# A transformer block on one core: a ninth unit of maxima beside the projections, no fourth bank of maxima in the attention, two V tiles later, five buffers of V rows

## The chip, the core and the metric

The kernel runs on one core of a Trainium2 chip. The core has a matrix engine (TensorE, PE in the profile; PEld is its weight load), a vector engine (VectorE, DVE), an activation engine (ScalarE, ACT), a general engine (GpSimd, POOL), and SyncE (SP), which here issues DMA transfers. ScalarE's queue issues a few more. The metric is the device time of one execution in microseconds (us); less is better.

## The reference

A transformer block over x of 2048 tokens by 512, with 32 heads of 16 and a feed-forward width of 1792, all in float32:

```python
def _A_ref(x, wqkv, wo):                       # attention
    qkv = (x @ wqkv).reshape(B, S, 3, H, Dh).transpose(2, 0, 3, 1, 4)
    q, k, v = qkv[0], qkv[1], qkv[2]
    scores = jnp.einsum("bhqd,bhkd->bhqk", q, k) * Dh ** -0.5
    p = softmax(scores, axis=-1)
    o = jnp.einsum("bhqk,bhkd->bhqd", p, v)
    return o.transpose(0, 2, 1, 3).reshape(B, S, D) @ wo

def _B_ref(x, w1, b1, w2, b2):                 # feed-forward
    return gelu(x @ w1 + b1) @ w2 + b2

mod = (silu(c) @ w_mod).reshape(c.shape[0], 6, 1, -1)
sa, ca, ga, sb, cb, gb = (mod[:, i] for i in range(6))
h = layernorm(x) * (1 + ca) + sa
x = x + ga * _A_ref(h, A_wqkv, A_wo)
h = layernorm(x) * (1 + cb) + sb
x = x + gb * _B_ref(h, B_w1, B_b1, B_w2, B_b2)
```

The softmax needs the largest score of each row of queries before its exponentials.

## The kernel before

Every engine works through its own list in the order in which the code writes it down. A product of two float32 matrices is made from high and low parts, in three terms (`mm3`, L284 to L292): 12 matmuls for a tile of 128 by 512.

**Stages.** The loop over four blocks of 512 tokens (L504 to L538) is the first part. In each block it normalises the next block (`ln1`, `ln1_t`), projects K and then Q for the first quarter of the heads (`proj_qk` with k = 0), and projects V tiles in between (`proj_v`). Block 0 takes four V tiles, blocks 1 and 2 two each, one before and one after the transposes of `ln1_t`. The second part (L547 to L602) is a list of 32 items: the eight V tiles that are left (n = 0 to 7), then K and Q for k = 1 to 3 over the four blocks. The attention (L819 to L844) follows, and then the feed-forward part.

**Units and maxima.** A unit is one group of four heads (of 8 groups) and one block of queries: 32 units, u = 4 g + block. Each unit needs 64 banks of maxima before its own scores can be made. There are two ways to get them.

- In the second part, `visit` (L556) makes two slots of `pair_slot` (L405). The keys of tokens t and t + 512 are held as their sum and their difference (`kpm`), so that the larger of two scores is half of a sum and an absolute value. A V slot makes two matmuls and two absolute values on ScalarE (L424); a U slot makes two matmuls and two VectorE instructions that add and keep the maximum (L428). From item 6 (`FILL0`) each item calls `visit` five times between its matmuls. `NU1` = 8 units are made so, in 256 slots.
- In the attention, `next_max` (L455) makes one bank by a matmul (L400) and a VectorE reduction (L402). The bank comes from the ring `mx` of three banks.

**A step of the attention.** A unit has 16 steps over the keys, kc = 0 to 15. A step has four score matmuls with their exponentials (X, L816 and L817, from the ring `sc` of four banks), the PV matmuls of the step before (P, L649, into the single bank `pv`), and three banks of maxima (M), in one of two orders (`ORDER`, L43). At kc = 4 and 12 (`EXTRA`, L45) a fourth bank is put in, and it is taken from the ring `sc`. The last unit makes no maxima.

**The sums of K.** `proj_qk` makes them for k = 0 alone (L305 to L322): of an even block ScalarE keeps a copy of K (`k2`); of the odd block VectorE makes sum and difference (`pm`), ScalarE the high parts (`pmh`), and, in `rest`, GpSimd the low parts, and two stores go to DRAM. `rest` also stores the projection's own parts, and is called after the next projection's matmuls. Its stores are issued by `st[0]`: ScalarE's queue until item 1 of the second part, SP's from there.

**K tiles and queues.** Four SBUF tiles hold keys: kt0, kt1, kq0, kq1. In the second part kt0 and kt1 first hold the sums of groups 0 and 1 (`build_k` of `kpm_d`, six loads each; half of kt0's are issued at block 3's start and half after the first part). kq0 is loaded with group 0 at item 10. At item 20 kt0 is loaded with group 2, which the attention's first maxima need; kt1 takes group 1 and kq1 group 3 after the last item. `load_qm` loads a unit's queries for the maxima, `load_q` for the scores. `max_rows` sends a finished unit's maxima to DRAM one item or step later (four stores). All of these go through SP's queue in the order of the code.

**V rows.** ScalarE writes a V tile into one of three buffers `vst` (L332, L333), and `rest` stores it to DRAM.

Of the kernel before, what the change touches and what calls it, by code (L numbers as in the profile page):

```python
# [16 lines left out]
P = 128  # L17
# [17 lines left out]
NU1 = 8  # L35
# [9 lines left out]
EXTRA = {4: "m0", 12: "m1"}  # L45
# [5 lines left out]
def block_kernel(ctx: ExitStack, tc: tile.TileContext, x, wqkv, wo, w1, b1, w2, b2, c, w_mod, out):  # L51
# [39 lines left out]
    kpm_d = dram.tile([2, P, S], F32, name="kpm")  # L91
# [33 lines left out]
    vst = [vwpool.tile([P, NG, VG], F32, name=f"vst{i}") for i in range(3)]  # L125
# [171 lines left out]
    def proj_qk(b, k, w, fill=()):  # L297
        hi, lo = hT[b]
        ps = bank()
        mm3(ps, [w_hi[k][:, w, i] for i in range(KC)], [w_lo[k][:, w, i] for i in range(KC)],  # L300
            [hi[:, i] for i in range(KC)], [lo[:, i] for i in range(KC)], fill)
        parts = tpool.tile([P, 2, TB], FR, tag="parts", name="parts", bufs=4)
        ac.activation(parts[:, 0], ps, AF.Copy)
        ve.tensor_tensor(parts[:, 1], ps, parts[:, 0].bitcast(F32), op=ALU.subtract)
        pair = w and k == 0  # L305
        if pair and b % 2 == 0:
            k2[0] = apool.tile([P, TB], F32, tag="k2", name="k2")
            ac.activation(k2[0], ps, AF.Copy)
        if pair and b % 2:
            pm = [apool.tile([P, TB], F32, tag="h32", name="pm", bufs=3) for _ in range(2)]  # L310
            pmh = [tpool.tile([P, 2, TB], FR, tag="parts", name="pmh", bufs=4) for _ in range(2)]
            for i, op in enumerate((ALU.add, ALU.subtract)):
                ve.tensor_tensor(pm[i], ps, k2[0], op=op)
                ac.activation(pmh[i][:, 0], pm[i], AF.Copy)

        def rest():
            st[0].dma_start(qk_d[w][k][:, :, b * TB : (b + 1) * TB].rearrange("a p t -> p a t"), parts.bitcast(F32))
            if pair and b % 2:
                for i in range(2):
                    gp.tensor_tensor(pmh[i][:, 1], pm[i], pmh[i][:, 0].bitcast(F32), op=ALU.subtract)  # L320
                    t0 = (b - 1 + i) * TB
                    st[0].dma_start(kpm_d[:, :, t0 : t0 + TB].rearrange("a p t -> p a t"), pmh[i].bitcast(F32))  # L322

        return rest
# [67 lines left out]
    def max_bank(u, i, a, bk):  # L392
# [6 lines left out]
        ps = bk()  # L399
# [55 lines left out]
    def next_max(a, bk=bank_mx):  # L455

        u, i = divmod(mi[a], NM)
        if u == NG * NB:
            return []
        if i == 4 and u + 1 < NG * NB and u + 1 not in qmx:  # L460
            load_qm(u + 1)
        mi[a] += 1
        max_bank(u, i, a, bk)
        return [] if left[u] else [max_rows(u)]
# [39 lines left out]
    for b in range(NB):  # L504
        if b == NB - 1:
# [6 lines left out]
            build_k(kts[0], kpm_d, 0, 0, 2 * TB)  # L512
# [7 lines left out]
        proj(proj_qk, b, 0, 1)  # L520
        proj(proj_qk, b, 0, 0)
# [4 lines left out]
        proj(proj_v, *vitems.pop(0))  # L526
        ev = ln1_t(b + 1, xn)
        ev()
        proj(proj_v, *vitems.pop(0))
# [5 lines left out]
        if b == 0:  # L535
            proj(proj_v, *vitems.pop(0))
            proj(proj_v, *vitems.pop(0))
    build_k(kts[0], kpm_d, 0, 2 * TB, S)  # L538
# [23 lines left out]
    for n, (k, b, w) in enumerate(items):  # L562
# [3 lines left out]
        if n == 8:  # L566
            build_k(kts[1], kpm_d, 1)
# [12 lines left out]
        if n == nv + 12:  # L580
            load_k(2, kts[0])
# [10 lines left out]
        if n >= FILL0:  # L592
            fill = [lambda rest=rest: (rest(), visit())] + [visit] * 4
# [18 lines left out]
    load_k(1, kts[1])  # L612
# [206 lines left out]
    for s in range(NS):  # L819
# [5 lines left out]
        order = list(ORDER[s % 2])  # L825
        if kc in EXTRA:
            order.insert(2, EXTRA[kc])
        for tok in order if u < NU - 1 else ORDER_END:
# [5 lines left out]
            else:  # L834
                new += next_max(int(tok[1]), bank if tok[0] == "m" else bank_mx)
# [149 lines left out]
```

## Time and profile before

| | us |
|---|---|
| three runs | 1789.81, 1792.59, 1793.21 |
| median of the runs | 1792.59 |
| profiled execution, its own time | 1789.69 |
| span of the profiled execution | 1787.9 |
| first part, to the last matmul of block 3's Q | about 80.1 |
| six V tiles without maxima | 80.3 to 101.6 |
| 26 items with maxima | 101.6 to 293.3 |
| attention | 293.3 to about 1430 |
| feed-forward part | about 1430 to 1787.9 |

Busy time over the whole span: TensorE 1768.5 us (99%), VectorE 1436.3 (80%), ScalarE 1343.1 (75%), GpSimd 246.4 (14%). Shares over the whole span are means over stages with different limits, so a stage is read by its own windows. A row of a window gives the stretch, its length, each engine's busy time with the number of instructions, the clock that TensorE was granted (1.00 is full speed), the share of the DMA engines and what they moved. A row of the timeline gives start and length in us, engine, line, operation, what is written and read, and in brackets the engine's idle time before it and what ended that. Matmuls overlap, so their lengths are longer than their distance. A row SPq or ACTq is a queue that issues a transfer.

### The profile page before, as it was taken

The numbers are of one execution on the slowest core, as the hardware profiler recorded it, in microseconds if no ns is written. First come the engines' busy times: TensorE is split into PE (matmuls) and PEld (weight loads), VectorE is DVE, ScalarE is ACT, GpSimd is POOL, SyncE is SP. The second block draws the span as 40 slices with busy tenths as digits, with TensorE's granted clock in tenths as the row PEclk, the third lists the DMA queues.
The fourth block names the chain that finished last, engine by engine and source line by source line (L and its number), as shares of the span: only waits on it lengthen the run. The fifth ranks groups of instructions, "written<-read, shape, count | busy, mean of one in ns | idle before, by whom it ended". The sixth has DMA issues, their size and how long they took to land.

```text
span 1787.9 us, 29214 instructions
## 1 busy us (share of the span) xinstructions
PE 1768.5 (99%) x10554; PEld 917.2 (51%) x10554; DVE 1436.3 (80%) x2591; ACT 1343.1 (75%) x2552; POOL 246.4 (14%) x259
## 2 busy tenths in 40 slices
PE   8999999999999999999999999999999999999998
PEld 7755554434444434444444434434434478788887
DVE  6469999999898889898988988898897476838453
ACT  3468887999999999999999999999999722223222
POOL 3300000010000000000000000000002044546462
PEclk9999999999999999999999999999999999999999
DMA  8776445411300410400411101100113064333331
GB/s 282 243 149 152 94 137 106 90 35 44 64 23 24 78 28 23 80 28 22 73 26 31 38 23 28 44 23 17 35 51 105 30 183 135 124 82 107 106 118 47
DMA packets 122432, 139.97 MB, mean 78 GB/s; under 512 B 38736, under 2 KB 72528, under 8 KB 120528
## 3 DMA queue, kind: packets, MB, share of 16 engines
q1 hardware_dynamic: 117872, 129.10, 28.5%
q10 hardware_dynamic: 4416, 9.01, 1.4%
q8 instruction: 83, 1.36, 0.3%
q14 instruction: 61, 0.50, 0.1%
HBM read 104.28 MB, written 33.77 MB: 77 GB/s over the span
## 4 chain that ended last, share of the span: by engine, by line
PE 91%; DVE 3%; DMA 2%; issue 2%; POOL 1%; SPq 0%; ACT 0%; ACTq 0%; DVEq 0%; POOLq 0%
PE pv L649 28%; PE mx L400 20%; PE sc L816 14%; PE sc L290 14%; PE mx L883 5%; PE mx L417 5%; PE pv L883 2%; PE sc L756 1%; PE mx L756 1%; DVE glo L866 0%; POOL w2l L687 0%; PE sc L252 0%; DMA rb<-rden 0%; DMA qk<-parts 0%; DVE cp L428 0%
## 5 line engine op out<-in xcount | busy, mean ns | idle before, releaser
L817 ACT ACTIVATE p<-sc 128x512 f32<-128x512 f32 x2048 | 1054.8, 613 | 72.9 <-PE sc L816 43.0
L402 DVE TENSOR_REDUCE mxs<-mx 128x1 f32<-128x512 f32 x1475 | 934.3, 684 | 109.7 <-PE sc L816 73.6
L649 PE MATMUL pv<-p,vg 128*32 128x512 f32 x4096 | 546.8, 605 | 0.0
L816 PE MATMUL sc<-qst,kq 50*128 50x512 f32 x1024 | 294.7, 439 | 1.4 <-DVE mxf L428 1.4
L816 PE MATMUL sc<-qst,kt 50*128 50x512 f32 x1024 | 293.3, 435 | 0.0
L400 PE MATMUL mx<-kq,qmx 48*128 48x512 f32 x737 | 258.5, 429 | 0.2
L400 PE MATMUL mx<-kt,qmx 48*128 48x512 f32 x738 | 258.4, 428 | 0.1
L400 PEld LDWEIGHTS mx<-kt,qmx 48*128 48x128 f32 x738 | 122.4, 185 | 219.2 <-DVE mxs L402 200.6
L400 PEld LDWEIGHTS mx<-kq,qmx 48*128 48x128 f32 x737 | 121.7, 185 | 219.7 <-DVE mxs L402 199.4
L862 ACT ACTIVATE g<-sc,b_c 128x512 f32<-128x512 f32 x56 | 38.6, 690 | 237.2 <-PE sc L290 228.5
L428 DVE CUSTOM_DVE_ANT_0 cp<-mx,cp 128x512 f32<-128x512 f32 x256 | 164.0, 686 | 30.4 <-PE mx L417 26.1
L649 PEld LDWEIGHTS pv<-p,vg 128*32 128x32 f32 x4096 | 81.1, 108 | 173.0 <-issue 161.3
L441 POOL CAST m<-mn 128x16 fp32r<-128x16 f32 x32 | 6.5, 202 | 1174.8 <-DVE mn L435 1174.8
L424 ACT ACTIVATE cp<-mx 128x512 f32<-128x512 f32 x256 | 141.1, 597 | 32.6 <-PE mx L417 27.9
L816 PEld LDWEIGHTS sc<-qst,kq 50*128 50x128 f32 x1024 | 131.3, 185 | 40.6 <-ACT p L817 31.6
L816 PEld LDWEIGHTS sc<-qst,kt 50*128 50x128 f32 x1024 | 131.2, 185 | 20.7 <-ACT p L817 14.7
L866 DVE TENSOR_TENSOR glo<-g,ghi 128x512 fp32r<-128x512 f32 x56 | 60.0, 1072 | 94.8 <-ACT ghi L865 94.8
L417 PE MATMUL mx<-kt,qmx 48*128 48x512 f32 x512 | 100.7, 456 | 0.5 <-ACT cp L424 0.5
L685 POOL TENSOR_TENSOR w1l<-w1r,w1h 128x512 fp32r<-128x512 f32 x56 | 76.8, 1372 | 152.7 <-DVE w1h L684 151.2
L290 PE MATMUL sc<-hThi,w 128*128 128x512 f32 x256 | 83.6, 436 | 2.9 <-DVE hThi L258 2.9
L687 POOL TENSOR_TENSOR w2l<-w2r,w2h 128x512 fp32r<-128x512 f32 x56 | 81.2, 1449 | 6.5 <-DVE w2h L686 6.1
L417 PEld LDWEIGHTS mx<-kt,qmx 48*128 48x128 f32 x512 | 52.8, 184 | 50.6 <-issue 23.3
(150 smaller groups left out, 1694.5 us busy)
## 6 DMA issues: line engine op xcount, KB each, us to landing
w1r<-in_B_w_dram SPq DMA_DIRECT2D x56, 256.0 KB
w2r<-in_B_w_dram SPq DMA_DIRECT2D x56, 256.0 KB
qmx<-qk SPq DMA_DIRECT2D x192, 64.0 KB
qk<-parts SPq DMA_DIRECT2D x24, 512.0 KB
qst<-qk SPq DMA_DIRECT2D x192, 64.0 KB
wmod<-in_w_mod_dram SPq DMA_DIRECT2D x6, 1024.0 KB
kq<-qk SPq DMA_DIRECT2D x24, 256.0 KB
kt<-qk SPq DMA_DIRECT2D x24, 256.0 KB
```

Source lines behind the costliest of these rows:

```text
L290: te.matmul(ps, p, q, start=i == 0, stop=i == len(terms) - 1)
L400: te.matmul(ps, qmx[u][rows, p, qc * P : (qc + 1) * P], kst[u // NB][rows, p, kr * TB : (kr + 1) * TB], start=True, stop=True)
L402: ve.tensor_reduce(mxs[u][:, p, a, qc, kr : kr + 1], ps, axis=AX.X, op=ALU.max, negate=True)
L417: te.matmul(ps, qmx[u][rows, p, qc * P : (qc + 1) * P], kpm[u // NB][rows, p, t0 : t0 + TB], start=True, stop=True)
L424: ac.activation(vabs[n, a], ps, AF.Abs)
L428: ve.tensor_tensor_reduce(v, ps, v, -0.5, 3.0e38, ALU.add, ALU.min, mxs[u][:, p, a, qc, r : r + 1])
L649: te.matmul(cur_pv[0][32 * j : 32 * (j + 1)], vg[g][:, kc, j * VW : j * VW + 32], pt.pop((s, j)), start=kc == 0, stop=kc == NKC - 1)
L685: gp.tensor_tensor(alo, a, ahi.bitcast(F32), op=ALU.subtract)
L687: gp.tensor_tensor(blo, b, bhi.bitcast(F32), op=ALU.subtract)
L816: te.matmul(ps, k[r0 : r0 + KX, p, kc * P : (kc + 1) * P], q[r0 : r0 + KX, p], start=True, stop=True)
L817: ac.activation(pb, ps, AF.Exp, scale=SCALE)
L883: te.matmul(acc[qb][t], p[:, sl], q, start=f == 0 and n == 0, stop=f == NF - 1 and n == 2)
```

## The change

- `NU1` is 9: 288 slots in 144 visits. The extra calls of `visit` go to every item whose number is a multiple of 7, from 7 to 28. The last item spreads its visits as if there were two more.
- `EXTRA` and the bank argument are gone: each step of the attention has three maxima from `mx`.
- `V_A` gives block 0 three V tiles (one before the transposes, two after), block 1 two, block 2 one, after the transposes. The list of items grows to 34, ten of them V tiles, so all item numbers from `nv` move by two.
- `vst` has five buffers.
- `proj_qk` makes the sums of K for k = 0 and for k = 1. `kpm_d` becomes two DRAM tensors. `k2` and `pm` move to another pool with tags of their own.
- In block 3, K's `rest` runs at once, ahead of Q's projection, with its stores on SP's queue.
- kt0 is loaded with the sums of group 2 at item `nv` + 11 = 21, for unit 8. So group 2's own K goes into kt1, at item `nv` + 22 = 32, and group 1's into kt0 after the last item.

```diff
--- before.py
+++ after.py
@@ -32,7 +32,7 @@
 KR = 3 * DH
 KX = KR + 2
 NM = 32
-NU1 = 8
+NU1 = 9
 FILL0 = 6
 VISIT = 2
 OP0 = 1
@@ -42,7 +42,7 @@
 
 ORDER = ("X0 X1 M1 X2 M0 X3 P M1".split(), "X0 X1 X2 M0 M0 X3 P M1".split())
 
-EXTRA = {4: "m0", 12: "m1"}
+V_A = ((1, 2), (1, 1), (0, 1))
 ORDER_END = "X0 X1 X2 X3 P".split()
 SCALE = DH ** -0.5
 
@@ -88,7 +88,7 @@
 
     qk_d = [[dram.tile([2, P, S], F32, name=f"qk{w}{k}") for k in range(4)] for w in range(2)]
 
-    kpm_d = dram.tile([2, P, S], F32, name="kpm")
+    kpm_d = [dram.tile([2, P, S], F32, name=f"kpm{k}") for k in range(2)]
     o_d = [dram.tile([D, TB], F32, name=f"o{b}") for b in range(NB)]
     den_d = [dram.tile([H, TB], F32, name=f"den{b}") for b in range(NB)]
     rden_d = [dram.tile([H, TB], F32, name=f"rden{b}") for b in range(NB)]
@@ -122,7 +122,7 @@
     wslots = [wpool.tile([P, KC, D], FR, name=f"w{i}") for i in range(2)]
     vwcm, vwpool = pool("vwpool", side="right")
     vslots = [vwpool.tile([P, KC, D], FR, name=f"wv{i}") for i in range(2)]
-    vst = [vwpool.tile([P, NG, VG], F32, name=f"vst{i}") for i in range(3)]
+    vst = [vwpool.tile([P, NG, VG], F32, name=f"vst{i}") for i in range(5)]
     acm, apool = pool("apool", side="right")
     c_c = apool.tile([P, KC], F32, name="c_c")
     s_c = apool.tile([P, KC], F32, name="s_c")
@@ -302,15 +302,15 @@
         parts = tpool.tile([P, 2, TB], FR, tag="parts", name="parts", bufs=4)
         ac.activation(parts[:, 0], ps, AF.Copy)
         ve.tensor_tensor(parts[:, 1], ps, parts[:, 0].bitcast(F32), op=ALU.subtract)
-        pair = w and k == 0
+        pair = w and k < 2
         if pair and b % 2 == 0:
-            k2[0] = apool.tile([P, TB], F32, tag="k2", name="k2")
-            ac.activation(k2[0], ps, AF.Copy)
+            k2[k] = tpool.tile([P, TB], F32, tag="k2", name="k2", bufs=1)
+            ac.activation(k2[k], ps, AF.Copy)
         if pair and b % 2:
-            pm = [apool.tile([P, TB], F32, tag="h32", name="pm", bufs=3) for _ in range(2)]
+            pm = [tpool.tile([P, TB], F32, tag="pm", name="pm", bufs=2) for _ in range(2)]
             pmh = [tpool.tile([P, 2, TB], FR, tag="parts", name="pmh", bufs=4) for _ in range(2)]
             for i, op in enumerate((ALU.add, ALU.subtract)):
-                ve.tensor_tensor(pm[i], ps, k2[0], op=op)
+                ve.tensor_tensor(pm[i], ps, k2[k], op=op)
                 ac.activation(pmh[i][:, 0], pm[i], AF.Copy)
 
         def rest():
@@ -319,7 +319,7 @@
                 for i in range(2):
                     gp.tensor_tensor(pmh[i][:, 1], pm[i], pmh[i][:, 0].bitcast(F32), op=ALU.subtract)
                     t0 = (b - 1 + i) * TB
-                    st[0].dma_start(kpm_d[:, :, t0 : t0 + TB].rearrange("a p t -> p a t"), pmh[i].bitcast(F32))
+                    st[0].dma_start(kpm_d[k][:, :, t0 : t0 + TB].rearrange("a p t -> p a t"), pmh[i].bitcast(F32))
 
         return rest
 
@@ -389,14 +389,14 @@
 
     mi = [NU1 * NM, NU1 * NM]
 
-    def max_bank(u, i, a, bk):
+    def max_bank(u, i, a):
 
         if u not in left:
             mxs[u] = small.tile([P, 2, 2, 4, 4], F32, tag="mxs", name="mxs")
             left[u] = 2 * NM
         p, qc, kr = i // 16, (i // 4) % 4, i % 4
         rows = slice(a * 64, a * 64 + KR)
-        ps = bk()
+        ps = bank_mx()
         te.matmul(ps, qmx[u][rows, p, qc * P : (qc + 1) * P], kst[u // NB][rows, p, kr * TB : (kr + 1) * TB],
                   start=True, stop=True)
         ve.tensor_reduce(mxs[u][:, p, a, qc, kr : kr + 1], ps, axis=AX.X, op=ALU.max, negate=True)
@@ -452,7 +452,7 @@
 
         return rest
 
-    def next_max(a, bk=bank_mx):
+    def next_max(a):
 
         u, i = divmod(mi[a], NM)
         if u == NG * NB:
@@ -460,7 +460,7 @@
         if i == 4 and u + 1 < NG * NB and u + 1 not in qmx:
             load_qm(u + 1)
         mi[a] += 1
-        max_bank(u, i, a, bk)
+        max_bank(u, i, a)
         return [] if left[u] else [max_rows(u)]
 
 
@@ -509,7 +509,7 @@
             qmcm, qmpool = pool("qmpool")
             kpm[0], kpm[1] = kts
             load_qm(0)
-            build_k(kts[0], kpm_d, 0, 0, 2 * TB)
+            build_k(kts[0], kpm_d[0], 0, 0, 2 * TB)
         if b == 2:
             split_w(1)
             load_w(2)
@@ -518,24 +518,27 @@
         if b + 2 < NB:
             load_x(b + 2)
         proj(proj_qk, b, 0, 1)
+        if b == NB - 1:
+            st[0] = sy
+            rest()
+            rest, st[0] = lambda: None, ac
         proj(proj_qk, b, 0, 0)
         if b == NB - 1:
             break
         if b in (1, 2):
             mrow = mod_rows(wms)
-        proj(proj_v, *vitems.pop(0))
+        for _ in range(V_A[b][0]):
+            proj(proj_v, *vitems.pop(0))
         ev = ln1_t(b + 1, xn)
         ev()
-        proj(proj_v, *vitems.pop(0))
+        for _ in range(V_A[b][1]):
+            proj(proj_v, *vitems.pop(0))
         if b == 1:
             mod_cols(1, mrow)
             wms = [load_wm(2, 0), load_wm(5, 1)]
         if b == 2:
             mod_bcast((ga_b, gb_b), mrow)
-        if b == 0:
-            proj(proj_v, *vitems.pop(0))
-            proj(proj_v, *vitems.pop(0))
-    build_k(kts[0], kpm_d, 0, 2 * TB, S)
+    build_k(kts[0], kpm_d[0], 0, 2 * TB, S)
     open_psum(sc=2, mx=6)
 
     vg = {}
@@ -564,7 +567,7 @@
             close(acm)
             st[0] = sy
         if n == 8:
-            build_k(kts[1], kpm_d, 1)
+            build_k(kts[1], kpm_d[0], 1)
             for t in kts:
                 one_rows(t)
         if n == nv + 1:
@@ -577,8 +580,11 @@
         if n == nv + 2:
             load_k(0, kq[0])
             load_v(0)
-        if n == nv + 12:
-            load_k(2, kts[0])
+        if n == nv + 11:
+            kpm[2] = kts[0]
+            build_k(kts[0], kpm_d[1], 2)
+        if n == nv + 22:
+            load_k(2, kts[1])
         if n == nv + 18:
             load_q(0)
         if n == nv + 20:
@@ -590,7 +596,9 @@
         new = []
         fill = [rest]
         if n >= FILL0:
-            fill = [lambda rest=rest: (rest(), visit())] + [visit] * 4
+            fill = [lambda rest=rest: (rest(), visit())] + [visit] * (4 + (n % 7 == 0))
+        if n == len(items) - 1:
+            fill += [lambda: None] * 2
         rest = proj_qk(b, k, w, fill) if k else proj_v(b, w, fill)
         for f in todo[:1]:
             f()
@@ -609,7 +617,7 @@
     pcm, ppool = pool("ppool", bufs=2)
     kq.append(ppool.tile([P, 2, S], FR, name="kq1", bufs=1))
     one_rows(kq[1])
-    load_k(1, kts[1])
+    load_k(1, kts[0])
     load_k(3, kq[1])
     epool = ctx.enter_context(tc.tile_pool(name="epool", bufs=1, side="right"))
 
@@ -822,17 +830,14 @@
         if kc == 2 and 0 < u < NU - 1:
             load_q(u + 1)
         new = []
-        order = list(ORDER[s % 2])
-        if kc in EXTRA:
-            order.insert(2, EXTRA[kc])
-        for tok in order if u < NU - 1 else ORDER_END:
+        for tok in ORDER[s % 2] if u < NU - 1 else ORDER_END:
             if tok[0] == "X":
                 exp_step(s, int(tok[1]))
             elif tok[0] == "P":
                 if s:
                     pv_step(s - 1)
             else:
-                new += next_max(int(tok[1]), bank if tok[0] == "m" else bank_mx)
+                new += next_max(int(tok[1]))
         for f in todo[:1]:
             f()
         todo = todo[1:] + new
```

## The prediction

> **What bounds the kernel now.** I read the chain of waits first, then a table of windows by stage.
>
> ```profile
> PE 91%; DVE 3%; DMA 2%; issue 2%; POOL 1%; SPq 0%; ACT 0%; ACTq 0%; DVEq 0%; POOLq 0%
> PE pv L649 28%; PE mx L400 20%; PE sc L816 14%; PE sc L290 14%; PE mx L883 5%; PE mx L417 5%; PE pv L883 2%; PE sc L756 1%; PE mx L756 1%; DVE glo L866 0%; POOL w2l L687 0%; PE sc L252 0%; DMA rb<-rden 0%; DMA qk<-parts 0%; DVE cp L428 0%
> ```
>
> ```profile
> core 0: us, PE busy (x) PEld busy (x) DVE busy (x) ACT busy (x) POOL busy (x), PEclk, DMA share, GB/s
> 0.00:40.00 40.00, 34.61 (x178) 27.51 (x179) 26.58 (x58) 13.15 (x21) 14.31 (x34) 0.91 0.87 304
> 40.00:75.00 35.00, 34.32 (x179) 24.52 (x178) 19.31 (x42) 15.12 (x25) 11.53 (x10) 1.00 0.63 224
> 75.00:102.50 27.50, 24.67 (x100) 19.32 (x98) 2.58 (x4) 6.40 (x11) 3.21 (x3) 0.94 0.77 215
> 102.50:293.30 190.80, 188.93 (x823) 100.88 (x822) 179.95 (x550) 155.69 (x287) 8.01 (x18) 1.00 0.51 123
> 293.30:330.00 36.70, 36.56 (x237) 14.84 (x239) 31.50 (x52) 32.84 (x64) 0.42 (x2) 0.95 0.91 130
> 330.00:1360.00 1030.00, 1029.90 (x7084) 416.27 (x7080) 926.77 (x1518) 975.29 (x1904) 31.41 (x63) 1.00 0.18 39
> ```
>
> TensorE holds the end almost everywhere, with VectorE and ScalarE close behind (90% and 95% in the attention). So a stage is worth what its TensorE rhythm changes by. Four places matter: the first part (to 80.1 us), the six V tiles without maxima (80.3 to 101.6), the 26 items with maxima (to 293.3), and 31 of the attention's 32 units (to about 1395).
>
> The attention's rhythm is read from the starts of the PV matmuls in the timeline. One step holds a fourth bank:
>
> ```profile
> 601.46 1.06 PE L649 MATMUL pv<-p,vg 128*32 128x512 f32 x8
> ...
> 603.04 0.40 PE L400 MATMUL sc<-kq,qmx 48*128 48x512 f32 x1
> ...
> 603.68 0.18 PEld L816 LDWEIGHTS sc<-qst,kt 50*128 50x128 f32 x1 [0.37 <-ACT p L817]
> ...
> 604.11 1.06 PE L649 MATMUL pv<-p,vg 128*32 128x512 f32 x8
> ...
> 606.23 1.07 PE L649 MATMUL pv<-p,vg 128*32 128x512 f32 x8
> ...
> 608.34 1.07 PE L649 MATMUL pv<-p,vg 128*32 128x512 f32 x8
> ```
>
> A plain step takes 2.12 us (604.11 to 606.23 to 608.34), the one with the bank 2.65. The fourth maximum sits in one of the four score banks, so the last score matmul waits for ScalarE. Over the trace the median is 2.637 with it and 2.124 without: 0.513 us each.
>
> The stall among the six V tiles:
>
> ```profile
> 97.33 3.30 PE L290 MATMUL sc<-wv,hThi 128*128 128x512 f32 x8 [2.83 <-ACT vst L333]
> 100.43 1.52 PE L290 MATMUL sc<-wv,hTlo 128*128 128x512 f32 x4
> ```
>
> With three row buffers ScalarE waits 7.14 us for a V store, and TensorE stands for 2.83. Then it runs slowly: 3.30 and 1.52 us, where the tile before took 2.03 and 1.10.
>
> **The sum.**
>
> 1. *No fourth bank.* Steps 4 and 12 of 31 units lose it: 62 x 0.513 = **-31.8**. The regular slots carry it: 31 x 48 = 1488 for 23 x 64 = 1472 banks. Unit 31's last maximum comes 16 slots early (5.3 steps of 2.12, 11.3 us; before, 14 slots, about 10). Bounds: -15, if only a bank's own share of the chain returns (20% of 1787.9 over 1475 banks = 0.242 each), to -33. I take the measured difference of steps.
>
> 2. *Nine units.* 16 more visits and two more items in the second part. An item without maxima takes 2.80 us, one with five visits 7.38 on average (24 items, from 109.8 to 286.9), so a visit costs (7.38 - 2.80) / 5 = 0.916. 16 x 0.916 + 2 x 2.80 = **+20.3**. VectorE allows it: two maxima per visit start 0.61 apart, six visits and the split of 0.69 are 8.0, TensorE needs 8.3. Bounds: +19 (two more items at 7.38 and four extra visits, the empty visits of the old last item forgotten) to +24 (all at VectorE's mean of 1.47 a visit).
>
> 3. *Sums of K for k = 1.* Two items get two VectorE passes (L313, 682 ns each as x4 in 2.6) and two ScalarE copies; VectorE's 6.9 us becomes 8.2, above 7.38: +0.9 each, with two single copies hidden under ScalarE's 6.0 us of an item: **+1.8** (0 if the six banks of maxima absorb it, 3 if not). Four GpSimd subtracts (1.29 each, an idle engine), four 512 KB stores and six 256 KB loads lie on SP's queue. The loads go at item 21, when unit 3's last matmul (item 18) has freed kt0; they hold the queue as the load at 209.2 did (the queue moved 106 to 131 GB/s until 223.2, then 385). The next q tile behind them is needed some 20 us on: 0.
>
> 4. *Two V tiles leave the first part.* After block 0 the next K projection could start 2.80 earlier: its last hThi (38.18) and hTlo (39.56) come before the matmuls that read them. In block 1 everything up to mod_cols follows. In block 2 the transposes wait for the normalised rows, so ScalarE's chain moves only 0.8 through h32's buffers while TensorE is free 2.8 earlier, and the projection reads the last part 1.3 us in: 2.0. **-4.8** (-3.6 to -5.6). The matmuls were charged in 2.
>
> 5. *Five row buffers.* Idle 2.83 plus slow 1.27 + 0.42: **-4.5**. The next reuse is item 5's, 22.5 us after block 3's K projection starts; the store it needs landed at 96.67, 22.2 after. That is thin: bounds -2 to -4.6.
>
> 6. *K's stores of block 3 from SP instead of ScalarE.* They follow six kt0 loads on SP and are followed there by six more and the V stores. The pair stores waited for GpSimd at 81.8 and 83.1 anyway, so they start no later, and ScalarE no longer stands 3.0 us at 84.49, which nothing waited for. The first visit needs the second half of kt0, landed before 96.67 (22.2 after the projection's start), and comes 23 after: 0, though without that cover a visit waits.
>
> 7. *Group 2's K tile late.* It went to kt0 at item 20; now kt1 must be free, so it goes at item 32 of 34. There SP first sends unit 7's maxima, as at 207.45, and the loads at 209.20, 3.3 us into the item; at 120 GB/s 1.5 MB end 14.0 later, 17.3 in. The attention's first maximum is the second token to use it, in the first step, and all of TensorE stands behind it. It comes 7.3 + 6.6 to the last visit, 2.5 of VectorE's tail and 0.8 more: 17.2. I take **+1** (0 to 5, as two 512 KB stores may lie ahead). Late next are the stores of the last items, the other two K tiles and qmx of unit 10, issued about 331 at latest before and needed 46 us into the attention.
>
> Sum: -31.8 + 20.3 + 1.8 - 4.8 - 4.5 + 1 = **-18.0**. The profiled execution took 1789.69 (span 1787.9 and 1.8 around it), so 1771.7. That is the lowest of the four times shown (1789.69, 1789.81, 1792.59, 1793.21; mean 1791.3, median of the runs 1792.59). I name **1773**, the mean less 18.
>
> On the clock: after the gap at 94.5 the windows show 0.59 granted from 97.3 to 101.5, and 0.85 and 0.71 at the attention's start, after a gap of 1.4. [...]
>
> **Rivals.**
>
> A. *The start of the attention takes the gain.* Term 7 grows: the K tile 5 us late, a half clock after it (1.7, as at 97.33), and unit 10's queries another 3. Then 1791.3 - 18 - 1 + 9.7 = 1782. For it: one queue carries all, its share was 0.91 here. Against: the loads go two items ahead. 15%.
>
> B. *Only a bank's streaming returns.* Term 1 is 62 x 0.242 = -15 and the sum -1.2: 1790, no change. For it: the wait on ScalarE could move to another score matmul. Against: thirteen neighbouring steps at 2.12 show none. 6%. [...]
>
> C. *ScalarE sets the unit: slower.* It is busy 33.3 of 35.17 us in a unit; if the two long steps are where it catches up, plain steps stretch and a unit stays at 35.17. The other terms are +13.8: 1805. It decides once a unit stays above 34.73 (13.8 / 31 = 0.44 below now). Against: in the last unit, without maxima, PV starts are 1.96 apart (1402.93, 1404.89), so ScalarE needs under 2.0 a step. 7%.
>
> **How the numbers follow.** The forecast has 72%, by itself 1766 to 1779 from its bounds. A (15%) is still faster; B is the case of no change, C of slower. 1.5% of A's cases reach no change. The range takes in A's 1782: 1765 to 1784. A measurement here can tell about 0.2% (3.6 us) from no change. Faster 0.86, same 0.07, slower 0.07.
>
> **What would show it.** PV starts 2.12 apart in steps 4 and 12, and units of 34.1 instead of 35.17. No gap and full clock among the V tiles; block 3's K projection near 69.7 instead of 74.45. 28 items with maxima, 7.4 us each, 8.3 where there are six visits, about 214 us in all instead of 191.7. TensorE's wait for the kt load at the attention's first maximum, 0 to 5 us. The prediction is wrong if plain steps grow beyond 2.15, or an item beyond 7.7.

## The result and the profile after

The changed kernel took 1810.43 us (median of 4 runs, 1805.58 to 1815.72), the kernel before 1792.9 (1789.81 to 1793.95). The ratio is 1.0101, interval 1.007 to 1.0132: slower by one per cent, where 1773 was forecast. The profiled execution took 1810.16 us, its span is 1808.4. The ratios below are to the kernel before, run alongside; an execution more than 1.5% above the fastest of its kernel (1862.36 and 1824.22 below) is not in them, though it is in the medians. Line numbers are those of the changed kernel; the same code stands up to some ten lines away from its place before.

First the chain of waits of the kernel after:

```profile
PE 91%; DVE 3%; DMA 2%; issue 2%; POOL 1%; SPq 1%; ACT 1%; DVEq 0%; POOLq 0%; ACTq 0%
PE pv L657 28%; PE mx L400 19%; PE sc L290 15%; PE sc L824 13%; PE mx L417 6%; PE mx L888 5%; PE pv L888 2%; PE sc L764 1%; DMA kt<-qk 1%; PE mx L764 1%; DVE glo L871 0%; POOL w2l L695 0%; DMA wmod<-in_w_mod_dram 0%; DMA rb<-rden 0%; PE sc L252 0%
```

It hardly differs from the one before: still 91% TensorE. What has changed is not who is waited for, but how fast TensorE runs. The table of windows by stage shows that (columns as before: stretch, length, busy time and count of each engine, granted clock, DMA share, GB/s):

```profile
70.50:93.00 22.50, 22.50 (x96) 17.62 (x95) 3.03 (x6) 7.06 (x13) 3.85 (x3) 1.00 0.85 221
93.00:150.00 57.00, 55.75 (x238) 28.40 (x236) 49.39 (x149) 45.48 (x87) 3.36 (x6) 1.00 0.70 134
150.00:222.00 72.00, 69.91 (x205) 32.39 (x205) 48.29 (x144) 40.76 (x78) 5.86 (x8) 0.62 0.41 122
...
333.30:370.00 36.70, 34.41 (x227) 14.10 (x231) 29.44 (x49) 31.89 (x62) 0.42 (x2) 0.91 0.93 163
370.00:1340.00 970.00, 970.00 (x6818) 386.15 (x6810) 864.25 (x1411) 946.34 (x1848) 20.24 (x51) 1.00 0.19 39
1340.00:1376.00 36.00, 32.41 (x191) 12.13 (x187) 26.04 (x46) 26.41 (x53) 10.49 (x10) 0.86 0.20 64
```

The first row is the V tiles: the stall is gone, TensorE is busy all the time at full clock. The third row is the one to look at. TensorE counts as 97% busy from 150 to 222, but it made 205 matmuls in 72 us, while in the row above it made 238 in 57. The granted clock, 0.62, is the column that tells why. VectorE and ScalarE have room there (48 and 41 of 72 us), so neither sets the pace. The last row holds a second loss, late in the attention.

In both profiles the record of the granted clock shows 1.00 and 0.50 alone, with edges on a grid of 3.41 us. After the start of the kernel it was at 0.50 from 97.9 and from 295.9, for 3.41 us each, in the kernel before; in the kernel after from 153.1 (27.31 us), 194.1 (27.31), 334.0 (6.83), 1358.0 (10.24) and 1569.7 (3.41).

The attention's rhythm is what was forecast. PV starts in the timeline of the kernel after, at the same place as before:

```profile
600.54 1.07 PE L657 MATMUL pv<-p,vg 128*32 128x512 f32 x8
...
602.68 1.06 PE L657 MATMUL pv<-p,vg 128*32 128x512 f32 x8
...
604.81 1.06 PE L657 MATMUL pv<-p,vg 128*32 128x512 f32 x8
```

No step of 2.65 is left: the first of these held the fourth bank before, and they are 2.14 and 2.13 us apart. The median of the steps that had it is 2.13, of all steps 2.12, and a unit takes 34.12 us instead of 35.17.

What comes ahead of the first two long stretches, in the timeline of the kernel after:

```profile
148.02 0.69 DVE L304 TENSOR_TENSOR parts<-sc,parts 128x512 fp32r<-128x512 f32 x1
...
148.63 1.28 DVE L313 TENSOR_TENSOR pm<-sc,k 128x512 f32<-128x512 f32 x2
...
149.82 0.68 DVE L428 CUSTOM_DVE_ANT_0 cp<-mx,cp 128x512 f32<-128x512 f32 x1
...
150.57 1.10 PE L417 MATMUL mx<-kt,qmx 48*128 48x512 f32 x2 [1.31 <-DVE mxf L428]
...
153.15 1.22 PE L290 MATMUL sc<-hTlo,w 128*128 128x512 f32 x2
```

VectorE makes the split of K (L304) and then both sums for k = 1 (L313) in one piece of 1.9 us. No maximum is made meanwhile, no bank of `mx` comes free, and TensorE stands 1.31 us. From 153.1 on its clock is halved: two matmuls of L290 span 1.22 us, at full clock 0.72. Block 3's sums do the same at 193.97 (a stop of 1.40, clock down from 194.1). From first matmul to first matmul the six items affected took 11.2, 13.8 and 11.0 us, then 12.7, 12.4 and 10.0, instead of 7.3 (8.4 for the second, which has six visits): some 26 us lost.

The loss in unit 29, in the timeline of the kernel after (an SPq row issues transfers; its length is the time of issuing):

```profile
1344.03 1.73 SPq L448 DMA_DIRECT2D m<-mt  x4
...
1349.69 1.26 SPq L381 DMA_DIRECT2D qst<-m  x2
...
1351.05 5.85 SPq L739 DMA_DIRECT2D rb<-rden  x4
...
1355.04 1.26 POOL L742 TENSOR_TENSOR o_b<-o_b,rb 128x512 f32<-128x512 f32 x1 [14.46 <-DMA rb<-rden]
...
1356.33 0.43 DVE L743 CAST kt<-o_b 128x512 fp32r<-128x512 f32 x1 [3.96 <-POOL o_b L742]
...
1357.42 0.49 PE L400 MATMUL mx<-kq,qmx 48*128 48x512 f32 x1 [3.41 <-DVE mxs L402]
```

SP stores the maxima of unit 30 and then issues the load that reads them back (L381), which goes only when the store has landed: 3.9 us in which SP issues nothing. The reciprocal sums `rb` of the output's normalisation stand behind it. GpSimd waits for them, VectorE's cast (L743) waits for GpSimd, VectorE's maxima stand behind the cast, and TensorE waits 3.41 us for a bank. Then its clock is halved for 10.24 us. The unit took 43.36 us instead of 34.2.

### The profile page after: what moved, and what is told of

Same layout as the page of the kernel before. It is cut to its first block, busy times and chain, and to the rows that moved or that the text cites. A ratio compares the mean times of both kernels' runs of the same rounds, so it can differ in the third digit from the quotient of the medians.

```text
span 1808.4 us, 29238 instructions
## 1 busy us (share of the span) xinstructions
PE 1782.5 (99%) x10554; PEld 912.8 (50%) x10554; DVE 1421.2 (79%) x2595; ACT 1362.0 (75%) x2590; POOL 251.7 (14%) x273
## 4 chain that ended last, share of the span: by engine, by line
PE 91%; DVE 3%; DMA 2%; issue 2%; POOL 1%; SPq 1%; ACT 1%; DVEq 0%; POOLq 0%; ACTq 0%
PE pv L657 28%; PE mx L400 19%; PE sc L290 15%; PE sc L824 13%; PE mx L417 6%; PE mx L888 5%; PE pv L888 2%; PE sc L764 1%; DMA kt<-qk 1%; PE mx L764 1%; DVE glo L871 0%; POOL w2l L695 0%; DMA wmod<-in_w_mod_dram 0%; DMA rb<-rden 0%; PE sc L252 0%
## 5 line engine op out<-in xcount | busy, mean ns | idle before, releaser
L824 PE MATMUL sc<-qst,kq 50*128 50x512 f32 x1024 | 286.5, 439 | 1.6 <-DVE mxf L428 1.6
L824 PE MATMUL sc<-qst,kt 50*128 50x512 f32 x1024 | 282.3, 431 | 0.0
L400 PE MATMUL mx<-kq,qmx 48*128 48x512 f32 x768 | 264.5, 431 | 3.7 <-DVE mxs L402 3.4
L400 PE MATMUL mx<-kt,qmx 48*128 48x512 f32 x704 | 240.9, 429 | 2.3 <-DMA kt<-qk 2.3
L428 DVE CUSTOM_DVE_ANT_0 cp<-mx,cp 128x512 f32<-128x512 f32 x288 | 185.4, 687 | 50.8 <-PE mx L417 45.0
L424 ACT ACTIVATE cp<-mx 128x512 f32<-128x512 f32 x288 | 157.5, 598 | 56.7 <-PE mx L417 54.8
L824 PEld LDWEIGHTS sc<-qst,kq 50*128 50x128 f32 x1024 | 127.1, 187 | 33.0 <-ACT p L825 22.9
L824 PEld LDWEIGHTS sc<-qst,kt 50*128 50x128 f32 x1024 | 125.6, 185 | 10.0 <-ACT p L825 3.1
L417 PE MATMUL mx<-kt,qmx 48*128 48x512 f32 x576 | 126.4, 495 | 3.6 <-DVE mxf L428 2.9
L290 PE MATMUL sc<-hThi,w 128*128 128x512 f32 x256 | 93.2, 474 | 3.3 <-DVE hThi L258 3.3
```

What stands on the lines that cost most here:

```text
L290: te.matmul(ps, p, q, start=i == 0, stop=i == len(terms) - 1)
L400: te.matmul(ps, qmx[u][rows, p, qc * P : (qc + 1) * P], kst[u // NB][rows, p, kr * TB : (kr + 1) * TB], start=True, stop=True)
L417: te.matmul(ps, qmx[u][rows, p, qc * P : (qc + 1) * P], kpm[u // NB][rows, p, t0 : t0 + TB], start=True, stop=True)
L424: ac.activation(vabs[n, a], ps, AF.Abs)
L428: ve.tensor_tensor_reduce(v, ps, v, -0.5, 3.0e38, ALU.add, ALU.min, mxs[u][:, p, a, qc, r : r + 1])
L824: te.matmul(ps, k[r0 : r0 + KX, p, kc * P : (kc + 1) * P], q[r0 : r0 + KX, p], start=True, stop=True)
```

## The experiments

**The two VectorE passes in the kernel before.** The sums for k = 1 are added to the kernel before, without the ninth unit. They are stored, and nothing reads them.

```diff
-        pair = w and k == 0
+        pair = w and k < 2
...
-                ve.tensor_tensor(pm[i], ps, k2[0], op=op)
+                ve.tensor_tensor(pm[i], ps, k2[k], op=op)
...
-                    st[0].dma_start(kpm_d[:, :, t0 : t0 + TB].rearrange("a p t -> p a t"), pmh[i].bitcast(F32))
+                    st[0].dma_start(kpm_d[k][:, :, t0 : t0 + TB].rearrange("a p t -> p a t"), pmh[i].bitcast(F32))
```

> The kernel before, with the sums of K for k = 1 made on VectorE as in the changed kernel and stored, but never read; eight units, the fourth bank and everything else as before. Theory (VectorE's two passes in an item halve the clock): two half-clock stretches of about 27 us appear after items 10 and 14, and the time rises by 20 to 28 us, to about 1815. Rival (the ninth unit's visits are needed for it, or the clock has another cause): no stretch, and the two items cost 0.9 us each: about 1794.5.

Measured: 1824.4 (1814.68 to 1862.36, 5 runs), ratio 1.0155 (1.0127 to 1.0182). The profiled execution is the longest of the five. In its timeline:

```profile
145.46 1.11 PE L417 MATMUL mx<-kt,qmx 48*128 48x512 f32 x2 [1.45 <-DVE mxf L428]
```

Half clock follows from 148.0 for 27.31 us, and after the second pair (a stop of 1.20 at 190.17) from 192.4 for 122.88 us. That second stretch is from this one long execution. The other four are not profiled, but their mean granted clock is on record: 0.974 to 0.984, against 0.991 to 0.996 for the kernel before alongside. So the sums alone cost what the whole change costs and more; neither the ninth unit nor the banks of the attention are needed for it.

**The sums on GpSimd.** In the kernel after, ScalarE copies K for k = 1 to SBUF, and GpSimd makes sum and difference from the copy.

```diff
+            if k:
+                ac.activation(pm[1], ps, AF.Copy)
             for i, op in enumerate((ALU.add, ALU.subtract)):
-                ve.tensor_tensor(pm[i], ps, k2[k], op=op)
-                ac.activation(pmh[i][:, 0], pm[i], AF.Copy)
+                if k == 0:
+                    ve.tensor_tensor(pm[i], ps, k2[k], op=op)
+                    ac.activation(pmh[i][:, 0], pm[i], AF.Copy)
...
                 for i in range(2):
+                    if k:
+                        gp.tensor_tensor(pm[i], pm[1], k2[k], op=(ALU.add, ALU.subtract)[i])
+                        gp.tensor_copy(pmh[i][:, 0], pm[i])
```

> The changed kernel, with the sums and differences of K for k = 1 made by GpSimd from a ScalarE copy, so that VectorE makes no passes for them. Theory: after each of the two items in which VectorE made these passes TensorE stood 1.3 to 1.4 us and its clock was halved for 27.3 us (153.1 to 180.4 and 194.1 to 221.4 us of the changed kernel's trace); these items and the next took 26.5 us more than items at full clock. Without the passes neither half-clock stretch appears and the time falls from 1810 to about 1784. Rival: the clock falls because 144 visits keep the second part denser as a whole, whoever makes the sums; then the stretches stay, and the time stays within 3 us of 1810.

Measured: 1803.66 (1799.25 to 1806.75), ratio 1.0057 (1.0036 to 1.0078). That is 20 us above the forecast. The stops behind the pair items are gone, but another took their place. In the timeline of this kernel:

```profile
139.57 12.73 SPq L157 DMA_DIRECT2D wraw<-in_A_wqkv_dram  x2
...
157.84 0.60 ACT L303 ACTIVATE parts<-sc 128x512 fp32r<-128x512 f32 x1 [2.23 <-DMA qk<-parts]
...
158.98 0.98 PE L423 MATMUL mx<-kt,qmx 48*128 48x512 f32 x2 [1.73 <-ACT cp L430]
```

The ring `parts` has four buffers, and a pair takes two of them. Its oldest store stands on SP behind loads that hold the queue for 12.73 us (the weights, behind group 0's keys), so ScalarE waits 2.23 us for a buffer, TensorE 1.73, and half clock follows from 160.8 for 34.13 us. The cause was removed, the effect came back from another wait.

**The normalisation three steps later.** In the kernel after, so that the loads of `rb` and the instructions that wait for them come three steps later, when the load of the maxima no longer holds SP for long.

```diff
-                at(s0 + (12 if qb else 6) + 2 * k + d, lambda qb=qb, k=k, i=i: o_norm(qb, k)[i]())
+                at(s0 + (12 if qb else 9) + 2 * k + d, lambda qb=qb, k=k, i=i: o_norm(qb, k)[i]())
```

> The changed kernel, with the normalisation of the first query block's attention output begun three steps later in unit 29. Theory: unit 29 took 43.4 us instead of 34.1 because the first load of reciprocals stands on SP's queue behind a load of maxima that waits for its store; VectorE and then TensorE wait for it, 3.4 us, and TensorE has half its clock for 10.2 us. Three steps later the queue is free: unit 29 at 34.2, the time lower by about 9 us, about 1801. Rival: the load is late because its own source is late (the reciprocals' store), or VectorE's queue is overfull there; then the stall moves with it and the time stays.

Measured: 1811.35 (1802.19 to 1813.18), ratio 1.0092 (1.0065 to 1.0118). The stop in unit 29 and the half clock at 1358 are gone, as the theory says, but the time is the same: half clock lasted 30.72, 27.31 and, at the start of the attention, 23.89 us instead of 6.83. (The loads of `rb` still follow the load of the maxima on SP, at 1362.17 and 1360.81, but nothing waits long for them now.) The wait there for group 2's K tile is 2.12 us against 2.29. By the time alone this run would have spoken against the theory; only the clock's record tells the two effects apart.

**Both together.**

> Both edits together: if the two causes are the whole of the difference to the forecast, 1810 - 26.5 - 9.2 = about 1774 to 1775, below the kernel before (1792.9). If they are not, it stays above 1785.

Measured: 1795.54 (1782.42 to 1802.62, 10 runs), ratio 1.0004 (0.9981 to 1.0026). The forecast was missed by 20 us: the stop for a buffer of `parts` remains (1.87 us at 160.20, then 30.72 us of half clock), and 17.07 us follow the start of the attention.

**And the loads out of the way.** As the last one, with the loads of group 0's keys and V rows moved from before the weights to item 25, and group 2's key load one item earlier.

```diff
-        if n == nv + 2:
+        if n == nv + 15:
             load_k(0, kq[0])
...
-        if n == nv + 22:
+        if n == nv + 21:
             load_k(2, kts[1])
```

> Sums of k = 1 on GpSimd, the normalisation three steps later, and two loads moved: group 0's K and V from item 12 to item 25, group 2's K from item 32 to item 31. In the run with the first two edits TensorE still stood 1.87 us at 160.2 (ScalarE waited for a store of K that stood behind loads on SP's queue) and 2.10 us at 327.6 (group 2's K tile), and had half its clock for 30.7 and 17.1 us after these. Theory (any stop of more than about a microsecond among the items costs a long half-clock stretch): both stops and both stretches go; what stays is the stop of 1.6 us at the attention's start with one or two windows of 3.4 us. Time about 1771 to 1776, faster than the kernel before by 1%. Rival (the stretches come from the load of the second part as such): half clock appears again without a stop, and the time stays near 1790.

Measured: 1778.59 (1777.74 to 1784.76), ratio 0.9927 (0.9911 to 0.9942): faster than both kernels. In its windows, the items and the start of the attention:

```profile
150.00:222.00 72.00, 71.39 (x301) 37.01 (x300) 67.28 (x206) 59.03 (x111) 16.18 (x20) 1.00 0.48 125
...
306.00:343.00 37.00, 35.37 (x199) 14.27 (x199) 28.93 (x55) 28.05 (x55) 0.42 (x2) 0.82 0.89 140
```

301 matmuls in the 72 us that held 205, at full clock. What is left is 13.65 us of half clock from 309.9, at a stop of 1.60 us for VectorE's last maxima. One or two windows of 3.41 us of it were in the forecast; the other two or three cost up to 3.4 or 5.1 us, if half of their length is lost, more than the 2.6 by which the median lies above it.

**Lateness or work?** Everything so far could also be put down to more work for VectorE in the items. So the sums go back to VectorE, in the kernel of the last run, from ScalarE's copy: once both at once behind the projection (burst), once one after each of the next item's first two visits (split). The instructions are the same, only their places differ.

```diff
             if k:
                 ac.activation(pm[1], ps, AF.Copy)
+                for i in range(2):
+                    ve.tensor_tensor(pm[i], pm[1], k2[k], op=(ALU.add, ALU.subtract)[i])
```

That is burst. In split the passes go into a function that `visit` calls, one `i` per call; in both, GpSimd's part and the stores are in it:

```diff
+        def k_sum(i):
+            ve.tensor_tensor(pm[i], pm[1], k2[k], op=(ALU.add, ALU.subtract)[i])
+            gp.tensor_copy(pmh[i][:, 0], pm[i])
...
                     if k:
-                        gp.tensor_tensor(pm[i], pm[1], k2[k], op=(ALU.add, ALU.subtract)[i])
-                        gp.tensor_copy(pmh[i][:, 0], pm[i])
+                        late.append(lambda i=i: k_sum(i))
+                        continue
...
         led += VISIT
+        if late:
+            late.pop(0)()
```

> all_fixes with the two sums of K for k = 1 made by VectorE instead of GpSimd (from ScalarE's copy), both at once behind the projection's subtract, in the items of blocks 1 and 3. Theory (a stop of TensorE of over a microsecond in the items costs it its clock): behind the projection VectorE is busy some 0.69 + 2 x 0.65 = 2.0 us, the next items' maxima come late, TensorE stops 0.8 to 1.3 us in each of the two following items, and half clock lasts 10 to 30 us after one or both; 1778.6 plus 10 to 27: 1789 to 1806. Rival (VectorE's total work sets these items, so it is the work and not where it lies): plus 1 us each, 1780 to 1782, and fixes_sums_split shows the same time.

> The same two VectorE sums as in fixes_sums_burst, but one after the first and one after the second visit of the next item, so that each lies between two pairs of maxima. Theory: each pass makes the maxima at most 0.65 us late, which six banks of maxima take up; no stop of over a microsecond and no half clock in the items; 1778.6 plus 0 to 2: 1778 to 1781. Rival (total work): the same time as fixes_sums_burst, whichever that is.

Measured: burst 1807.03 (1791.89 to 1811.1, 6 runs), ratio 1.0063 (1.0028 to 1.0097); split 1780.64 (1779.28 to 1799.14, 10 runs), ratio 0.995 (0.9928 to 0.9972). The timeline of burst, where half clock follows from 155.6 for 27.31 us:

```profile
151.85 1.42 DVE L316 TENSOR_TENSOR pm<-pm,k 128x512 f32<-128x512 f32 x2 [0.66 <-ACT pm L314]
...
152.36 0.99 PE L432 MATMUL mx<-kt,qmx 48*128 48x512 f32 x2 [0.63 <-ACT cp L439]
```

The same work costs 28 us in one place and 2 in another, so it is the place. The mean granted clock of all executions agrees: 0.974 to 0.986 for burst, 0.991 to 0.996 for nine of the ten of split, 0.992 to 0.996 for the kernel with all fixes. The stop is only 0.63 us here, less than the theory asked for. VectorE had first waited 0.66 us for ScalarE's copy, and the maxima behind its passes come late one by one: the next four, at 154.17, take 1.58 us instead of 0.73.

The profiled execution of split is the one at 1799.14. It has half clock for 61.44 us from 142.3, with no stop longer than 0.31 us ahead:

```profile
141.06 0.98 PE L431 MATMUL mx<-kt,qmx 48*128 48x512 f32 x2 [0.31 <-ACT cp L438]
...
153.08 0.69 DVE L321 TENSOR_TENSOR pm<-pm,k 128x512 f32<-128x512 f32 x1
```

The second row is the first of the moved passes. It comes 10.8 us after the clock fell, so this loss is not theirs. Ahead of the fall ScalarE copies parts of the next weights, which the kernel with all fixes does at the same place, with a wait of 0.29 us and no loss. The other nine executions lie between 1779 and 1786. So no loss of the split order is seen, but the theory, which asks for a stop of over a microsecond, does not explain this one.

**One or two idle passes.** In the kernel before, one or two VectorE passes that nothing reads, behind the K projection of item 24. The diff is that with two.

```diff
+        if (k, b, w) == (3, 0, 1):
+            junk = tpool.tile([P, TB], F32, tag="junk", name="junk", bufs=1)
+            for _ in range(2):
+                ve.tensor_tensor(junk, ps, parts[:, 0].bitcast(F32), op=ALU.add)
```

> The same with one pass. Theory: VectorE is 0.65 us late, the six banks and TensorE's own spare time take most of it, TensorE stands under 0.8 us, no half-clock stretch: within 2 us of 1793.8. If one pass is enough, the time rises as with two.

> The kernel before with nothing but two more VectorE passes at the end of item 24 (their result is not used), as long as the sums of K, far from loads. Theory: TensorE stands 1.2 to 1.4 us in item 25, the clock is halved for 20 us or more, and the time rises by 10 us or more (from 1793 to 1803 or above). Rival (the half clock needs the loads or the stores that come with the sums): no stretch, the time within 2 us of 1793.8.

Measured: one pass 1794.05, ratio 1.0008 (0.9999 to 1.0017), no change; two passes 1803.28 (1796.19 to 1824.22, 6 runs), ratio 1.0059 (1.0035 to 1.0084). The profiled execution with two passes (1802.07) has no half clock among the items. The delay is there: the four maxima from 248.63 came late one by one and took 1.79 us instead of 0.73, the item took 1.1 us more, but the clock stayed. Half clock came at the attention's start only, for 17.07 us instead of 3.41. So the profiled execution does not show the step expected. The mean granted clock of the six executions runs from 0.993 (the shortest) to 0.975 (the longest), against 0.993 to 0.998 for the kernel before alongside; where it fell in the other five is not on record.

**Two passes, then dense matmuls.** As with two passes, and items 26 and 27 have no visits; their ten visits follow item 27 in one piece. So VectorE's burst is followed first by full matmuls alone, then by those of the maxima alone.

```diff
+        if n in (26, 27):
+            fill = [rest]
...
+        if n == 27:
+            for _ in range(10):
+                visit()
```

> Two passes at the end of item 24, and items 26 and 27 without visits between their matmuls; their ten visits follow item 27. Theory: the clock is not given back while short matmuls of maxima (48 rows) and full ones alternate, but is by one window of 3.4 us of unbroken full matmuls; 24 of these take 10 us at half clock and hold such a window, so the stretch ends within item 27, 10 to 17 us after it began instead of 27. The ten visits without cover cost about 3 us themselves. Rival (the stretch has a fixed length): still 27 us.

Measured: 1815.25 (1804.04 to 1823.58, 4 runs), ratio 1.0122 (1.0085 to 1.016). Windows of this kernel, cut where the clock changes:

```profile
249.60:256.40 6.80, 6.80 (x19) 3.66 (x18) 4.41 (x13) 3.10 (x6) 0.42 (x2) 0.50 0.29 77
256.40:266.70 10.30, 9.21 (x40) 5.35 (x38) 6.10 (x18) 5.75 (x10) 0.00 (x0) 1.00 0.42 142
266.70:276.00 9.30, 9.09 (x28) 4.37 (x26) 7.71 (x26) 6.93 (x13) 0.00 (x0) 0.50 0.16 59
276.00:314.50 38.50, 38.50 (x100) 17.47 (x98) 22.79 (x68) 18.83 (x35) 0.42 (x2) 0.50 0.14 46
```

The first row is the loss behind the two passes. Up to item 26 the code is that of the run with two passes, and so is the delay (four late maxima from 247.57, no wait over 0.20 us): there the clock stayed, here it fell. The clock was back after 6.8 us, the last 2.7 of them with full matmuls alone (from 253.66). It fell again at 266.7, amid the ten visits, and stayed down through them (third row) and on through ordinary items (fourth row: 100% busy, 2.6 matmuls a microsecond; 4.3 in the items of the kernel before).

**What all the profiles say together.** The time of a profiled execution, less half of its time at half clock (between 40 and 1750 us), worked out from the records of the clock:

```
                          half clock  profiled  less half of it
before                          6.83   1789.69    1786.3
before_one_pass                13.65   1794.69    1787.9
before_two_passes              23.89   1802.07    1790.1
before_two_passes_dense        78.51   1823.58    1784.3
before_with_k1_sums           163.84   1862.36    1780.4
after                          75.09   1810.16    1772.6
norm_later                     85.33   1813.18    1770.5
sums_gpsimd                    68.27   1806.75    1772.6
sums_gpsimd_norm_later         51.20   1797.64    1772.0
all_fixes                      13.65   1778.99    1772.2
fixes_sums_burst               85.33   1809.27    1766.6
fixes_sums_split               71.68   1799.14    1763.3
```

Times from 1779 to 1813 become 1770.5 to 1772.6 for five of the seven variants of the kernel after. Half of the length is an estimate, from the 0.50 of the record: all work of the stretch would take twice as long. In the items less was lost: the one of the kernel after that lies wholly at half clock took 13.8 us instead of 8.4, 5.4 more and not 6.9. So with long stretches among the items the subtraction takes off too much (the last two rows, and the fifth). Within either family, then, nearly all of the differences are the clock. The mean granted clock, which is on record for every execution, says the same of those without a profile. Taking off span times (1 - clock) brings the 47 executions of the kernel before, and those of its four variants that count, to between 1780 and 1787, and the ten with both edits together, measured from 1782 to 1803, to between 1763 and 1771. The kernel after lies some 14 us below the one before in the reckoning of the table (1772.6 against 1786.3), so most of the gain that was forecast is in it, under the half clock.

## Why the prediction was wrong, by its own steps

| step | forecast | measured |
|---|---|---|
| 1 no fourth bank | -31.8 | -32.4 (first to last PV -23.2, without unit 29's loss) |
| 2 and 3, item 6 to the attention | +22.1 | +49.3 (191.5 to 240.7), some 26 of it in six items at half clock |
| 4 and 5, start of item 6 | -9.3 | -9.2 (101.79 to 92.55) |
| 7 group 2's K tile | +1 | +2.4 (wait 2.29, at half clock) |
| unit 29 | none | +9.2 |
| feed-forward part | none | +1.3 |
| sum | -18.0 | +20.5 (the terms above are rounded) |

*Steps 1, 4, 5 and 6* hold, and step 2 nearly. Block 3's Q was taken from PSUM at 76.28 instead of 80.90 (-4.6 of the -4.8 of step 4), and no visit waited for the second half of kt0. Without the loss of the six items the second part grew by some 23.3, where step 2 has 20.3. Part of the difference is that the single copies of `k2` were not hidden under ScalarE's work: the item behind one took 8.1 us, not 7.3.

*Step 3 is the one that failed.* It priced the two passes as VectorE's time, "+0.9 each", with nothing as the best case, if the six banks absorb it. The delay was of that size: TensorE stood 1.31 and 1.40 us. What was missing is the half clock that followed these stops, 27.31 us each time. The prediction had seen the effect twice: 0.59 granted from 97.3, after a stop of 2.83 us, and 0.85 and 0.71 at the attention's start, after one of 1.4 us, the length of the stops that came. It took the effect into step 5 and rival A as 1.7 us, for a stretch of 3.41 us, and into step 3 not at all. It did not ask how long half clock would last in another place. Among the V tiles of the kernel before, where TensorE made full matmuls alone, it lasted 3.41 us (from 97.9); among the items of the kernel after it lasted 27.31 us, twice. The prediction's own sign of being wrong, an item beyond 7.7 us, came in these six. The kernel before with the sums alone (1824.4 us), and burst against split (1807.03 against 1780.64), show that the place of these two passes decides it.

*The second miss lies in step 1's sentence "the regular slots carry it".* That is true, and it also moves the end of a unit's maxima. With 9 units made ahead the maxima of unit 30 end at about step 5 of unit 29 instead of step 7, so their store and the load that reads it back come ahead of the `rb` loads on SP. Step 6 and 7 looked at the queue in the second part, and none looked at it in the attention. With `norm_later` the stop is gone, and unit 29 takes 34.7 us: 3.41 us of stop and 10.24 us at half clock (5.1) are 8.5 of the 9.2.

*The rivals.* A's place was right and its size wrong: the wait for the K tile was 2.29 us, with 6.83 us at half clock. In the timeline of the kernel after:

```profile
333.28 0.50 PE L824 MATMUL sc<-qst,kq 50*128 50x512 f32 x2 [1.60 <-DVE mxf L428]
...
336.07 0.76 PE L400 MATMUL mx<-kt,qmx 48*128 48x512 f32 x1 [2.29 <-DMA kt<-qk]
```

The clock fell at 334.0, when TensorE had stood 1.60 us for VectorE's last maxima and had only begun to wait for the tile. The kernel with all fixes has that stop, and half clock from it on, without a wait for the tile, so the tile need not have brought it. B and C fell: units take 34.12 us, below C's point of 34.73. The side was C's, the mechanism not.

*On the clock.* It fell after stops of 0.63 us (burst) to 3.41 us (unit 29 of the kernel after), and in two executions (split from 142.3, two passes with dense matmuls from 249.6) with no wait over 0.31 us ahead. It stayed at half for 27.31 us, eight steps of the grid of 3.41 us, while TensorE counts as busy throughout (27.25 of 27.25 us from 153.15 in the kernel after).

What stays open: why the same lateness behind item 24 cost the clock in one profiled execution and not in another, and why the attention's start takes 3.41 us of half clock in one kernel and 23.89 in another. No run separates where on the grid of 3.41 us a stop falls from how long it is.

## What to carry to other kernels

Where TensorE is 97% busy and a stage is still slow, read the granted clock and the number of matmuls before any chain of waits: here two stops of 1.31 and 1.40 us cost some 26 us together. Spread added work on an engine that feeds TensorE so that no piece is longer than the buffers ahead of it (split took 1780.64 us, burst 1807.03), and price its lateness by what the clock does in that stage, not by its own time. And when a producer gets faster, look at what its stores and loads now come ahead of on each queue, stages later too.

## What the hardware showed that was not expected

*Half clock followed windows with few matmuls, none of them idle.* I counted the matmuls that start in each 3.41-us window of the grid (in units of 512 columns), in all twelve profiles, between 80 and 430 us, and asked whether the next window was at half clock:

```
starts in a full-clock window      up to 10    11 to 13    14 and more
windows                                29          76          919
next one at half clock                 26           4            0
```

Each of the 29 holds three matmuls or more. At full clock an ordinary window of the items holds 14 to 16; by that a stop of a microsecond takes four or five of them away, an estimate. The windows of the two stops in the kernel after hold 9 each (from 149.7 and 190.7). Some of the windows of 11 to 13 are those where ScalarE's copies at an item's end hold TensorE for some 0.3 us; the split run's stretch began after one with 12, and so did that amid the ten visits of the dense run. Three windows with 8 to 10 matmuls kept the clock, so the count alone does not decide it.

*Among the items of these profiles it came back only after windows with four or more full-height matmuls.* In the items' half-clock windows (134 in these profiles, between 105 and 290 us) I counted the matmuls of 128 rows and those of 48 rows. With four or more of 128 rows, 11 of 58 windows were the last at half clock; with three or fewer, none of 76, whatever the number of 48-row ones (up to 10) and though TensorE counts as busy throughout. That fits 6.8 us in the dense stretch against 27 us and more in the mixed items. It is not shown as the cause: it is a count over windows, 47 of the 58 did not bring the clock back, and no run changed the rows alone.
